# Hash-masked attention and a ReLU MLP on one core: value casts and sums leave GpSimd, row sums come out of the scaling, squares go to ScalarE

## The chip, the cores and the metric

The kernel runs on one core of a Trainium2 chip. Its engines are TensorE (PE in the profile; its weight loads are PEld), VectorE (DVE), ScalarE (ACT), GpSimd (POOL) and SyncE (SP), which only issues DMAs here. The metric is the device time of one execution in microseconds (us). The time before is 297.56 us, the median of three runs (296.8 to 298.05).

## The reference

The inputs are q, k and v of shape (4 batches, 8 heads, 768, 64), a projection to 6 hash bits, and the weights of an MLP (512 to 2048 to 512). A query sees a key only where all six hash bits agree.

```python
q_bits = (np.einsum('bhsd,dk->bhsk', q, proj) > 0)      # and k_bits likewise
mask = q_bucket[:, :, :, None] == k_bucket[:, :, None, :]
scores = np.where(mask, scale * np.matmul(q, k.transpose(0, 1, 3, 2)), -1e9)
attn = np.exp(scores - np.max(scores, axis=-1, keepdims=True))
attn = attn / (np.sum(attn, axis=-1, keepdims=True) + 1e-09)
attn_out = np.matmul(attn, v)
...
x = attn_out.transpose(0, 2, 1, 3).reshape(B, S, H * D)
xn = (x - mu) / np.sqrt(var + 1e-06) * g_ln             # mu, var over the 512 of a row
out = x + np.maximum(xn @ w_ch1, 0.0) @ w_ch2
```

## The kernel before

The work is cut into 12 units. Unit u is a third (256 rows) of the queries of batch u // 3, and has two groups g of four heads. All 768 keys are taken at once, in six blocks of 128. The code is a set of small functions, one for each step, and a long table ORDER of words such as `na.v.5.0`: step, engine (t TensorE, v VectorE, a ScalarE, p GpSimd, s SyncE), arguments (the unit, then the group or part). The program is the table read from left to right; each engine runs its own words in that order, one behind the other, and waits by semaphores for what it reads. A second table, SLOTS, gives each tile its buffer. So a word that waits holds everything behind it on its engine.

The steps, with their lines in the profile:

- Queries and keys of batches 1 to 3: `LX` loads them, `tu` turns them in 32x32 blocks (VectorE, L326), `CA` casts them to bf16 (L333 on ScalarE, L335 and L337 otherwise). `hm` projects them on TensorE (L547), `bt` makes bits of it (L329), and `mw` and `mr` send the bits through DRAM into tile G. Before, the keys' casts (`CA.p`, with 1 as the last argument) run on GpSimd.
- Values of a batch: `lv` loads them, `cv` casts them into vaug beside a column of ones (L495 or L497), `su` adds them over the key blocks in three passes (L502 to L504, GpSimd), `sp` sums that over the partitions with a matmul (L509), and `sc` copies the result into vsB (L522, L524).
- Attention: `S` multiplies the bits and then q and k (TensorE, L603), `E` takes the exponential (ScalarE, L620), `A` multiplies with the values (TensorE, L631). On VectorE, `na` adds a tiny multiple of the value sums (L643) and so frees the PSUM tile; `nb` takes the reciprocal of the row sum (L650) and scales (L652).
- Layer norm: `nc` takes the statistics (L656) and `ag` joins them (L659), both on VectorE; `rs` makes 1/sqrt of the variance on GpSimd, in two tiny instructions (L670, L671); `ce` subtracts and scales into xc (L665); `fl` is the transposing DMA into xnT (L674, SP's queue).
- First MLP product, in one of two ways. Plain (units 0 to 4 and 11): `F` on TensorE, eight parts of 8 matmuls that are 256 wide (L694), each evicted with the Relu by `R` (L702 on ScalarE, L704 on VectorE). By block products (units 5 to 10): `bs` adds input blocks (L736), `M` runs 14 parts of 8 matmuls that are 128 wide (L760), and `V` (L769, L771), `U` (L778), `Q` (L782, L784) and `ru` (L790, L792) combine the results on ScalarE and VectorE. These products need four sums of weight blocks, made once by `w1s` (L723).
- Second MLP product: `D` and `Z` in unit 0 (L797, L800), else by seven products `P` (L849) with input sums `ss` (L834) and additions `Y` to x (L854). `O` sends x out on SP's queue (L868; the last unit's at L866 also from ScalarE's).

PSUM has three two-bank tiles (tag pp) that S, A and unit 10's wide M share, and two one-bank tiles (tag f) for all else.

Of the kernel before, what the change touches and what calls it, by code (L numbers as in the profile page):

```python
# [38 lines left out]
tu.v.1.1.0.3 E.a.2.0.0.1 A.t.1.1.0.0 A.t.1.1.0.1 CA.p.1.0.1 na.v.1.1 nb.v.1.1 mr.s.1.0.2 mr.s.1.0.0  # L39
tu.v.1.1.0.1 tu.v.1.1.0.2 E.a.2.0.0.0 nc.v.1.0 F.t.0.2 R.a.0.2 S.t.2.0.2 S.t.2.0.3 E.a.2.0.1.1 su.p.1.0  # L40
# [17 lines left out]
tu.v.2.0.0.3 CA.a.2.0.0 Y.v.1.5 ss.v.1.3 S.t.4.0.2 ss.v.1.4 P.t.1.3 Y.v.1.6 Y.v.1.3 w1s.v.1.0 P.t.1.7 F.t.2.0
R.a.2.0 Y.v.1.7 nb.v.3.0 A.t.3.1.1.1 P.t.1.4 A.t.3.1.1.2 F.t.2.6 E.a.4.0.0.2 A.t.3.1.0.0 tu.v.2.0.1.1 Y.v.1.4
A.t.3.1.1.0 su.p.1.4 sp.t.1.4 E.a.4.0.0.0 A.t.3.1.0.2 A.t.3.1.0.1 nc.v.3.0 R.v.2.6 sc.a.1.4 na.v.3.1 nb.v.3.1  # L60
nc.v.3.1 ag.v.3.1 ag.v.3.0 F.t.2.2 R.v.2.2 S.t.4.0.3 N.a.4.0.1 S.t.4.0.4 E.a.4.0.1.1 S.t.4.0.5 O.s.0.3
E.a.4.0.1.2 hm.t.2.0 bt.v.2.0 E.a.4.0.1.0 O.s.1.0 CA.p.2.0.1 rs.p.3 ce.v.3.1 lv.s.2.0.0 O.s.0.1 lv.s.2.4.2
F.t.2.3 cv.a.2.0.0 ce.v.3.0 F.t.2.4 S.t.4.1.0 N.a.4.1.0 R.v.2.4 S.t.4.1.1 S.t.4.1.2 E.a.4.1.0.1 E.a.4.1.0.2
R.v.2.3 F.t.2.7 lv.s.2.4.0 O.s.1.1 R.a.2.7 F.t.2.5 fl.s.3.1 fl.s.3.0 O.s.1.3 A.t.4.0.0.1 A.t.4.0.1.0
E.a.4.1.0.0 LX.s.3.0.1 lv.s.2.4.1 lv.s.2.4.3 mw.s.2.0 O.s.1.2 tu.v.2.1.0.1 w1s.v.1.1 A.t.4.0.1.1 R.v.2.5
tu.v.2.1.0.0 ss.v.2.1 A.t.4.0.1.2 A.t.4.0.0.2 A.t.4.0.0.0 O.s.0.2 na.v.4.0 P.t.2.2 S.t.5.0.0 N.a.5.0.0
S.t.5.0.1 Y.v.2.2 S.t.5.0.2 E.a.5.0.0.1 E.a.5.0.0.2 E.a.5.0.0.0 P.t.2.1 ss.v.2.3 ss.v.2.2 F.t.3.6 Y.v.2.1
P.t.2.6 tu.v.2.1.1.0 ss.v.2.4 su.p.2.0 tu.v.2.1.1.3 R.v.3.6 S.t.4.1.3 N.a.4.1.1 S.t.4.1.4 E.a.4.1.1.1
S.t.4.1.5 tu.v.2.1.0.3 P.t.2.5 Y.v.2.6 P.t.2.7 Y.v.2.5 P.t.2.3 mr.s.2.0.1 Y.v.2.7 tu.v.2.1.1.2 E.a.4.1.1.0
# [119 lines left out]
def kernel(  # L189
# [16 lines left out]
    P = 128  # L206
# [706 lines left out]
```

## Time and profile before

| | |
|---|---|
| median of three runs | 297.56 us |
| the profiled execution, its own time | 299.32 us |
| its span on the core | 297.6 us |
| granted TensorE clock, mean | 0.999 |
| instructions in the profile, VectorE / ScalarE / GpSimd | 552 / 241 / 95 |
| chain that ended last: PE, DVE, issue, ACT, DMA | 74%, 17%, 3%, 3%, 1% |
| DMA traffic | 34.15 MB, mean 115 GB/s |

The busy line counts the time in which an engine runs something. Groups of instructions show line, engine, operation, out<-in, partitions x elements and type, their number, then the busy time in us and the mean of one in ns, and the idle time of the engine just ahead of them with what ended it. In the timeline each row is a run of equal instructions with start and length in us. TensorE's "idle" is time in which no matmul is under way.

### The profile page before, as it was taken

To read this page: it belongs to the slowest core of one execution; us is meant where nothing else is said; L and a number is where in the kernel's file an instruction comes from. 1 tells how busy PE (TensorE), PEld (TensorE's weight loads), DVE (VectorE), ACT (ScalarE), POOL (GpSimd) and SP (SyncE) were. 2 spreads that over 40 slices of the span, in tenths; PEclk is the share of its full clock that TensorE was granted. 3 is DMA by queue.
4 is the path that set the end of the run, shared out by engine and by line. 5 is a ranking of instruction groups with operands and counts; after the bars stand their busy time and mean duration, and the time that the engine had idled before them with its cause. 6 is when DMAs were issued, how large, how long until landed. Compare 5 with 4: busy or idle time off the path is not lost.

```text
span 297.6 us, 11168 instructions
## 1 busy us (share of the span) xinstructions
PE 282.2 (95%) x4879; PEld 227.9 (77%) x4879; DVE 247.8 (83%) x552; ACT 208.6 (70%) x241; POOL 64.8 (22%) x95
## 2 busy tenths in 40 slices
PE   8999999999999999999999999999899999977994
PEld 4777777558786885887887778788688879976883
DVE  4767899899988989999899898898698898986553
ACT  4789998987676755966766976887777985734140
POOL 4470415140511534202000235004101020010000
PEclk9999999999999999999999999999999999999999
DMA  6999896659905826417512022301200303012132
GB/s 198 367 288 269 190 276 115 135 176 175 326 16 144 240 63 220 103 29 195 150 32 68 12 70 65 73 3 37 55 20 20 71 22 56 4 35 63 24 111 72
DMA packets 31059, 34.15 MB, mean 115 GB/s; under 512 B 15521, under 2 KB 27809, under 8 KB 31010
## 3 DMA queue, kind: packets, MB, share of 16 engines
q1 hardware_dynamic: 25938, 28.72, 35.5%
q0 software_dynamic: 4224, 4.19, 8.6%
q8 instruction: 38, 0.62, 0.9%
q10 hardware_dynamic: 848, 0.53, 0.7%
q14 instruction: 11, 0.09, 0.1%
HBM read 27.86 MB, written 6.88 MB: 117 GB/s over the span
## 4 chain that ended last, share of the span: by engine, by line
PE 74%; DVE 17%; issue 3%; ACT 3%; DMA 1%; SPq 0%; POOL 0%; DVEq 0%; ACTq 0%
PE sc L603 14%; PE X L849 12%; PE f L694 11%; PE acc L631 10%; PE Yb L849 6%; PE Ma L760 6%; PE hf L415 3%; PE Me L760 3%; PE Ya L849 3%; ACT E L620 2%; PE hp L547 2%; PE Mae L760 2%; DVE xc L665 2%; DVE T L326 2%; DVE x L652 2%
## 5 line engine op out<-in xcount | busy, mean ns | idle before, releaser
L620 ACT ACTIVATE E<-sc,bias_sb 128x1024 bf16<-128x1024 f32 x144 | 152.4, 1115 | 39.6 <-PE sc L603 39.3
L603 PE MATMUL sc<-qb,kb 32*128 32x256 bf16 x1152 | 52.4, 267 | 0.0
L694 PE MATMUL f<-xnT,w_sb 128*128 128x256 bf16 x384 | 47.0, 273 | 1.2 <-DVE x L800 0.7
L603 PE MATMUL sc<-G 6*128 6x256 bf16 (+1 forms) x576 | 42.9, 272 | 2.6 <-ACT E L620 2.1
L694 PEld LDWEIGHTS <-w_sb 128*128 128x128 bf16 x384 | 36.0, 98 | 8.6 <-issue 4.8
L631 PE MATMUL acc<-vaug,E 128*128 128x65 bf16 x1152 | 42.3, 193 | 0.0
L631 PEld LDWEIGHTS <-E 128*128 128x128 bf16 x1152 | 40.2, 97 | 1.8 <-issue 0.4
L849 PEld LDWEIGHTS <-hb 128*128 128x128 bf16 x352 | 32.9, 98 | 8.3 <-issue 4.3
L603 PEld LDWEIGHTS <-kb 32*128 32x128 bf16 x1152 | 30.6, 93 | 1.3
L603 PEld LDWEIGHTS <-G 6*128 6x128 bf16 (+1 forms) x576 | 17.3, 91 | 16.9 <-issue 12.3
L849 PEld LDWEIGHTS <-S 128*128 128x128 bf16 x264 | 25.0, 98 | 5.3 <-issue 1.3
L702 ACT ACTIVATE hb<-f 128x512 bf16<-128x512 f32 x30 | 17.9, 601 | 15.6 <-PE f L694 14.2
L670 POOL TENSOR_SCALAR rs<-mv 128x2 f32<-128x2 f32 x12 | 3.0, 252 | 115.2 <-DVE mv L659 115.1
L326 DVE STREAM_TRANSPOSE T<-X 128x384 f32<-128x384 f32 (+2 forms) x52 | 26.4, 538 | 0.0
L643 DVE SCALAR_TENSOR_TENSOR y<-vsB,acc 128x520 f32<-128x520 f32 x24 | 16.6, 691 | 8.2 <-PE acc L631 7.4
L849 PE MATMUL Yb<-w_sb,S 128*128 128x256 bf16 x176 | 22.8, 273 | 0.5 <-DVE S L834 0.4
L854 DVE TENSOR_TENSOR x<-X,x 128x256 f32<-128x256 f32 x44 | 18.3, 419 | 5.1 <-PE X L849 4.5
L849 PE MATMUL X<-wt,hb 128*128 128x256 bf16 x168 | 21.8, 273 | 0.0
L652 DVE TENSOR_TENSOR x<-y,rc 128x512 f32<-128x512 f32 x24 | 20.1, 835 | 0.8
L760 PEld LDWEIGHTS <-Wx 128*128 128x128 bf16 x288 | 16.8, 98 | 4.0 <-issue 3.9
L760 PEld LDWEIGHTS <-w_sb 128*128 128x128 bf16 x288 | 16.9, 98 | 2.1 <-issue 2.0
L656 DVE BATCH_NORM_STATS2 st<-x 128x6 f32<-128x256 f32 x48 | 17.7, 412 | 0.2
(125 smaller groups left out, 433.9 us busy)
## 6 DMA issues: line engine op xcount, KB each, us to landing
out_dram<-x SPq DMA_DIRECT2D x45, 128.0 KB
X<-in_k_dram SPq DMA_DIRECT2D x7, 768.0 KB
vn<-in_v_dram SPq DMA_DIRECT2D x24, 192.0 KB
X<-in_q_dram SPq DMA_DIRECT2D x6, 768.0 KB
w_sb<-in_moe_w_ch_dram POOLq DMA_DIRECT2D x8, 512.0 KB, 11.0
vn<-in_v_dram SPq DMA_DIRECT2D x2, 768.0 KB
X<-in_q_dram SPq DMA_DIRECT2D x2, 512.0 KB
Bd<-B SPq DMA_DIRECT2D x6, 96.0 KB
```

The source lines that it names most:

```text
L326: nc.vector.transpose(d[:, j], s[:, j, kj0 : kj0 + n])
L603: m = nc.tensor.matmul(sc(u, g, a, p)[:, bank, 256 * half : 256 * half + 256], lh, rh, start=(rep == 0), stop=(rep == 2), skip_group_check ...
L620: nc.scalar.activation(Ep(u, g, a, p), sc(u, g, a, p), AF.Exp, scale=EXP_SCALE, bias=bias_sb)
L631: nc.tensor.matmul(acc[:, qt, (D + 1) * i : (D + 1) * (i + 1)], Ep(u, g, a, p)[:, bank, 256 * half + P * qt : 256 * half + P * qt + P], va ...
L643: nc.vector.scalar_tensor_tensor(yt(u, g), vs, EPS_ROW, made[f"acc{u}_{g}"][:, :, :A], op0=AOP.mult, op1=AOP.add,)
L652: nc.vector.tensor_tensor(xo, a[:, :, :, 0:D], rc.to_broadcast([P, 2, 4, D]), op=AOP.mult)
L656: nc.vector.bn_stats(stats(u)[:, qt, g], xt(u)[:, qt, 256 * g : 256 * g + 256])
L694: nc.tensor.matmul(f1[:, n].rearrange("p (t x) -> p t x", t=2), w1_sb[:, dt, P * nt : P * nt + P], xnT(u)[:, :, dt], start=(dt == 0), stop ...
L702: nc.scalar.activation(hb(u)[:, 2 * p : 2 * p + 2], f1, AF.Relu)
L760: nc.tensor.matmul(m[:, n], lh(kt)[:, P * nt : P * nt + P], rh[:, kt], start=(first and n == 0 and kt == 0), stop=(kt == 1), skip_group_ch ...
L849: nc.tensor.matmul(f2, lh[:, n], rh[:, n], start=(first and n == 0), stop=(n == 7), skip_group_check=True)
L854: nc.vector.tensor_tensor(x, made[f"{prod(u, k)}{u}"], x, op=AOP.add)
```

## The change

The kernel after does five things otherwise.

1. The key casts, value casts and value sums of batches 1 to 3 leave GpSimd. Of six key casts, three go to ScalarE and three to VectorE. Of the six value casts, the count on ScalarE rises from 4 to 10. All six value sums go to VectorE. GpSimd keeps batch 0's casts, the weight DMAs, the memsets of ones, and the tiny steps of the norm.
2. For units 3 to 11 the scaling `nb` becomes two scalar_tensor_tensor instructions that are 256 wide and also give each row's sum. `nc` and `ag` go for these units. A new step `mn` on GpSimd adds the two groups' sums and multiplies by -1/512, a new step `sv` on ScalarE squares x minus the mean and gives the sum of squares (what it writes into xc is overwritten by `ce`), and `rs` and `ce` read these.
3. Unit 4's first MLP product is made by block products: 40 parts F instead of 48, 98 parts M instead of 84.
4. Steps change engines: Relu evictions `R` go from 18 to 7 on VectorE and from 30 to 33 on ScalarE; `Q` from 1 to 7 on VectorE and 11 to 7 on ScalarE; `V` from 10 to 14 on VectorE and 26 to 28 on ScalarE; `U` on VectorE from 36 to 42.
5. ORDER and SLOTS are written anew from where unit 1's second half begins. The first 229 words are the same.

```diff
-tu.v.1.1.0.3 E.a.2.0.0.1 A.t.1.1.0.0 A.t.1.1.0.1 CA.p.1.0.1 na.v.1.1 nb.v.1.1 mr.s.1.0.2 mr.s.1.0.0
+tu.v.1.1.0.3 E.a.2.0.0.1 A.t.1.1.0.0 A.t.1.1.0.1 CA.a.1.0.1 na.v.1.1 nb.v.1.1 mr.s.1.0.2 mr.s.1.0.0
...
-WIDE = (10,)
+WIDE = {10}
+SUMS = 3
...
-        nc.vector.tensor_tensor(xo, a[:, :, :, 0:D], rc.to_broadcast([P, 2, 4, D]), op=AOP.mult)
+        if u < SUMS:
+            nc.vector.tensor_tensor(xo, a[:, :, :, 0:D], rc.to_broadcast([P, 2, 4, D]), op=AOP.mult)
+            return
+        for t in range(2):
+            nc.vector.scalar_tensor_tensor(
+                xo[:, t], a[:, t, :, 0:D], 1.0, rc[:, t].to_broadcast([P, 4, D]), op0=AOP.mult, op1=AOP.mult,
+                accum_out=rows(u)[:, g, t : t + 1],
+            )
+
+    def rows(u):
+        return sb(f"rw{u}", [P, 5, 2], F32, "rw", 3)
+
+    def mn(eng, u):
+        r = rows(u)
+        eng.tensor_tensor(r[:, 2], r[:, 0], r[:, 1], op=AOP.add)
+        eng.tensor_scalar(r[:, 3], r[:, 2], -1.0 / DM, None, op0=AOP.mult)
+
+    def sv(eng, u, t):
+        r = rows(u)
+        nc.scalar.activation(
+            xc(u)[:, t], xt(u)[:, t], AF.Square, bias=r[:, 3, t : t + 1], accum_out=r[:, 4, t : t + 1],
+        )
...
-        else:
+        elif u < SUMS:
...
+        else:
+            nc.vector.tensor_scalar(
+                xc(u)[:, t], xt(u)[:, t], rows(u)[:, 3, t : t + 1], rstd(u)[:, t : t + 1], op0=AOP.add, op1=AOP.mult,
+            )
...
-        nc.gpsimd.tensor_scalar(rstd(u), mv(u)[:, :, 1], 1e-6, None, op0=AOP.add)
+        if u < SUMS:
+            nc.gpsimd.tensor_scalar(rstd(u), mv(u)[:, :, 1], 1e-6, None, op0=AOP.add)
+        else:
+            nc.gpsimd.tensor_scalar(rstd(u), rows(u)[:, 4], 1.0 / DM, 1e-6, op0=AOP.mult, op1=AOP.add)
         nc.gpsimd.tensor_tensor(rstd(u), rstd(u), mhalf, op=AOP.pow)
```

In the rows below, a line number is that of the kernel the rows belong to (the one after is some 30 lines longer), and the number behind a name tells buffers of one name apart. First GpSimd's queue while batch 2 is made ready, before: key casts (kb), value sums (t, vsum) and value casts (vaug) of batch 2 stand between the norms (rs) of units 3 and 4.

```order
50 L337 CAST kb_2169<-T 128x1536
51 L670 TENSOR_SCALAR rs_2171<-mv_2097 128x2
52 L671 TENSOR_TENSOR rs_2171<-rs_2171,mhalf 128x2
53 L502 TENSOR_TENSOR t_2428<-vn_1820 128x512
54 L503 TENSOR_TENSOR t_2428<-t_2428,vn_1820 128x512
55 L504 TENSOR_TENSOR vsum_2431<-t_2428 128x256
56 L482 MEMSET vaug_2189 128x48
57 L483 MEMSET vsB_2639 128x8
58 L502 TENSOR_TENSOR t_2732<-vn_2178 128x512
```

The same queue after, from the norm of unit 3 on; rw is the new tile of row sums.

```order
40 L669 TENSOR_TENSOR rw_2039<-rw_2039 128x2
41 L670 TENSOR_SCALAR rw_2039<-rw_2039 128x2
42 L701 TENSOR_SCALAR rs_2190<-rw_2039 128x2
43 L702 TENSOR_TENSOR rs_2190<-rs_2190,mhalf 128x2
44 L485 MEMSET vaug_2193 128x48
45 L486 MEMSET vsB_2195 128x8
46 L669 TENSOR_TENSOR rw_2551<-rw_2551 128x2
47 L670 TENSOR_SCALAR rw_2551<-rw_2551 128x2
```

The wide passes are gone from it, and each norm has two more tiny ones ahead of the two that it had.

Second, ScalarE's queue while unit 6's scores come, before: E6 are unit 6's exponentials, hb4 the Relu evictions of unit 4's plain product, vsB2 a copy of value sums.

```order
114 L620 ACTIVATE E6_101_3189<-sc6_101_3153,bias_sb_66 128x1024
115 L702 ACTIVATE hb4_3167<-f1_44_3215 128x512
116 L702 ACTIVATE hb4_3167<-f1_45_3230 128x512
117 L702 ACTIVATE hb4_3167<-f1_47_3244 128x512
118 L702 ACTIVATE hb4_3167<-f1_46_3259 128x512
119 L702 ACTIVATE hb4_3167<-f1_40_3268 128x512
120 L620 ACTIVATE E6_102_3341<-sc6_102_3172,bias_sb_66 128x1024
121 L522 COPY vsB2_2639<-vp20_3304 128x4x64
122 L620 ACTIVATE E6_100_3368<-sc6_100_3150,bias_sb_66 128x1024
```

The same place after: kb30 is a key cast of batch 3, xc5 the squares of unit 5, and V4 are copies of unit 4's block products.

```order
126 L623 ACTIVATE E6_001_2997<-sc6_001_2945,bias_sb_66 128x1024
127 L336 ACTIVATE kb30_3021<-T_839 128x1536
128 L623 ACTIVATE E6_011_3128<-sc6_011_3103,bias_sb_66 128x1024
129 L623 ACTIVATE E6_012_3147<-sc6_012_3115,bias_sb_66 128x1024
130 L623 ACTIVATE E6_010_3177<-sc6_010_3100,bias_sb_66 128x1024
131 L674 ACTIVATE xc5_3218,rw5_3017<-x5_3016,rw5_3017 128x512
132 L800 COPY V460_3245<-Ma40_3166 128x512
133 L674 ACTIVATE xc5_3218,rw5_3017<-x5_3016,rw5_3017 128x512
134 L623 ACTIVATE E6_101_3265<-sc6_101_3195,bias_sb_66 128x1024
```

The evictions of unit 4 are gone from here, and the squares of unit 5 stand behind three exponentials and ahead of the next ones.

Third, VectorE's queue while batch 2's values are summed, after: t220 and vsum2 are the value sums, xc3 the normalised rows of unit 3, T the turned blocks of batch 2.

```order
143 L885 TENSOR_TENSOR x1_1008<-X1_1891,x1_1008 128x256
144 L329 STREAM_TRANSPOSE T_839<-X211_1750 128x384
145 L505 TENSOR_TENSOR t220_2165<-vn20_1657 128x512
146 L506 TENSOR_TENSOR t220_2165<-t220_2165,vn20_1657 128x512
147 L507 TENSOR_TENSOR vsum2_2168<-t220_2165 128x256
148 L754 TENSOR_TENSOR Wv1_2198<-w1_sb_75,Wx1_2015 128x1024
149 L693 TENSOR_SCALAR xc3_2142<-x3_2038,rw3_2039,rs3_2190 128x512 x2
150 L329 STREAM_TRANSPOSE T_839<-X210_2113 128x384 x2
```

The three passes of a value sum, before on GpSimd, now stand in VectorE's queue ahead of unit 3's normalised rows.

More of the change, by code (lines that the diff above doesn't have):

```diff
@@ new lines @@
+E.a.3.0.0.2 LX.s.2.0.1 mr.s.1.1.2 mr.s.1.1.0 nc.v.2.1 mr.s.1.1.3 D.t.0.0.2 D.t.0.1.1 D.t.0.1.2 D.t.0.1.3
+D.t.0.0.3 tu.v.2.0.0.0 mr.s.1.1.1 sw.v.3.0 ag.v.2.0 tu.v.2.0.0.2 ag.v.2.1 S.t.3.0.3 S.t.3.0.4 Z.v.0.0
+N.a.3.0.1 S.t.3.0.5 cv.a.1.0.0 lv.s.1.4.2 Z.v.0.1 E.a.3.0.1.1 F.t.1.1 R.a.1.1 wg.v.2 F.t.1.7 R.v.1.7
+E.a.3.0.1.0 F.t.1.0 E.a.3.0.1.2 rs.p.2 R.a.1.0 lv.s.1.4.1 F.t.1.6 lv.s.2.0.1 lv.s.1.4.0 tu.v.2.0.0.1 ce.v.2.1
+S.t.3.1.0 N.a.3.1.0 R.a.1.6 S.t.3.1.1 S.t.3.1.2 ce.v.2.0 w1s.v.1.1 tu.v.2.0.1.1 E.a.3.1.0.2 F.t.1.4
@@ new lines @@
+S.t.4.1.3 N.a.4.1.1 S.t.4.1.4 O.s.0.1 E.a.4.1.1.1 S.t.4.1.5 ss.v.2.4 tu.v.2.1.1.0 P.t.2.5 tu.v.2.1.0.1 Y.v.2.6
+ss.v.2.3 Y.v.2.5 P.t.2.7 su.v.2.4 mr.s.2.0.3 O.s.1.1 P.t.2.3 O.s.0.0 O.s.1.0 O.s.1.3 Y.v.2.3 E.a.4.1.1.0
+A.t.4.1.1.0 A.t.4.1.0.2 E.a.4.1.1.2 A.t.4.1.0.0 nb.v.4.0 A.t.4.1.1.1 A.t.4.1.1.2 A.t.4.1.0.1 na.v.4.1
+mr.s.2.0.2 Y.v.2.7 F.t.3.1 S.t.5.0.3 S.t.5.0.4 N.a.5.0.1 S.t.5.0.5 R.a.3.1 nb.v.4.1 w1s.v.3.1 mr.s.2.0.1
+E.a.5.0.1.2 P.t.2.4 Y.v.2.4 F.t.3.4 E.a.5.0.1.1 E.a.5.0.1.0 CA.v.2.1.1 hm.t.2.1 CA.v.2.1.0 cv.v.2.4.0
@@ new lines @@
+Y.v.6.6 cv.a.3.4.2 E.a.9.1.0.0 nb.v.8.1 P.t.6.3 P.t.6.7 A.t.9.0.0.1 A.t.9.0.1.2 A.t.9.0.1.0 Y.v.6.7 O.s.5.1
+bs.v.7.2 bs.v.7.4 Y.v.6.3 P.t.6.4 Y.v.6.4 bs.v.7.3 E.a.9.1.0.1 M.t.7.1.0 mn.p.8 sv.a.8.1 A.t.9.0.0.0
+A.t.9.0.0.2 A.t.9.0.1.1 V.a.7.1.0 na.v.9.0 M.t.7.2.0 U.v.7.1.0 M.t.7.6.0 S.t.9.1.4 S.t.9.1.3 sv.a.8.0
+V.a.7.6.0 nb.v.9.0 M.t.7.5.0 V.v.7.5.0 N.a.9.1.1 E.a.9.1.1.1 M.t.7.7.0 U.v.7.4.0 S.t.9.1.5 E.a.9.1.1.2
+M.t.7.3.0 U.v.7.2.0 E.a.9.1.1.0 M.t.7.4.0 S.t.10.0.0 N.a.10.0.0 Q.v.7.0 rs.p.8 ce.v.8.0 M.t.7.1.1 V.a.7.1.1
```

233 lines of the change are left out of this document (110 added, 123 removed).

## The prediction

> **What bounds the kernel now.** I read the page's busy line first, then the sums by stretch, then the timeline wherever TensorE stood still.
>
> ```profile
> PE 282.2 (95%) x4879; PEld 227.9 (77%) x4879; DVE 247.8 (83%) x552; ACT 208.6 (70%) x241; POOL 64.8 (22%) x95
> ...
> 40.00:260.00 220.00, 214.72 (x3924) 173.64 (x3917) 196.59 (x424) 165.18 (x188) 46.35 (x54) 1.00 0.40 97
> 88.00:153.00 65.00, 64.15 (x1085) 51.19 (x1084) 59.97 (x122) 44.76 (x52) 17.02 (x19) 1.00 0.49 135
> 260.00:276.00 16.00, 12.75 (x149) 11.22 (x147) 12.52 (x26) 6.11 (x10) 1.41 (x2) 1.00 0.23 50
> 276.00:293.30 17.30, 17.26 (x158) 15.18 (x156) 9.37 (x24) 4.79 (x8) 0.00 (x0) 1.00 0.21 56
> 293.30:297.60 4.30, 0.00 (x0) 0.00 (x0) 0.42 (x1) 0.00 (x0) 0.00 (x0) 0.96 0.44 119
> ```
>
> The columns behind each stretch are its length, then the busy time of TensorE's matmuls, of its weight loads, of VectorE, ScalarE and GpSimd, and the granted clock. TensorE is the bound: of the 220 us from 40 to 260 it is idle for 5.28, and from 276 until the last matmul for 0.04. VectorE is close behind, with 59.97 of 65 us busy from 88 to 153. ScalarE and GpSimd have room. So a gain has four possible sources: less TensorE work, the 5.28 us in the middle, the 3.25 us from 260 to 276, and the 4.30 us of output transfers at the end, which the change leaves alone. The first 40 us are the same in both kernels.
>
> **Who makes TensorE wait in the middle.** These are rows of the timeline: start, length, engine, line, operation; in brackets the idle time ahead of it and who ended that.
>
> ```profile
> 45.51 1.26 POOL L502 TENSOR_TENSOR t<-vn 128x512 f32<-128x512 f32 x1 [6.18 <-ACT E L620]
> 45.56 1.76 DVE L652 TENSOR_TENSOR x<-y,rc 128x512 f32<-128x512 f32 x1
> 52.57 1.50 PE L547 MATMUL hp<-T,p 128*32 128x384 f32 x16 [0.55 <-DVE T L326]
> 63.32 1.03 DVE L665 TENSOR_SCALAR xc<-x,mv,rs 128x512 bf16<-128x512 f32 x1
> 64.93 1.02 DVE L665 TENSOR_SCALAR xc<-x,mv,rs 128x512 bf16<-128x512 f32 x1
> 67.27 3.65 PE L694 MATMUL f<-xnT,w_sb 128*128 128x256 bf16 x32 [0.66 <-DVE x L800]
> 78.02 1.21 DVE L834 TENSOR_TENSOR S<-hb 128x1024 bf16<-128x1024 bf16 x1
> 79.89 0.38 PE L849 MATMUL X<-w_sb,hb 128*128 128x256 bf16 x2 [0.71 <-DVE hb L704]
> 110.31 1.54 DVE L652 TENSOR_TENSOR x<-y,rc 128x512 f32<-128x512 f32 x1
> 112.69 0.29 PE L603 MATMUL sc<-G 6*128 6x256 bf16 x4 [0.46 <-DVE y L643]
> 113.72 1.93 DVE L652 TENSOR_TENSOR x<-y,rc 128x512 f32<-128x512 f32 x1
> 116.17 1.03 PE L694 MATMUL f<-xnT,w_sb 128*128 128x256 bf16 x8 [0.23 <-DVE B L329]
> 176.06 1.75 DVE L834 TENSOR_TENSOR S<-hb,S 128x1024 bf16<-128x1024 bf16 x1
> 177.86 1.05 PE L849 MATMUL Yb<-w_sb,S 128*128 128x256 bf16 x8 [0.36 <-DVE S L834]
> L652 DVE TENSOR_TENSOR x<-y,rc x24: 691/692/1934, 24.4 to 256.6; 128x512 f32<-128x512 f32 x24
> L665 DVE TENSOR_SCALAR xc<-x,mv,rs x22: 501/541/1090, 59.7 to 266.3; 128x512 bf16<-128x512 f32 x22
> L834 DVE TENSOR_TENSOR S<-hb,S x12: 415/682/1748, 83.0 to 289.3; 128x1024 bf16<-128x1024 bf16 x10, 128x512 bf16<-128x512 bf16 x2
> ```
>
> The last three rows give minimum, median and maximum of one operation in ns. The same VectorE instruction takes 692 ns at the median and 1.54 to 1.93 us in these places, and in each of them a GpSimd sum or cast runs beside it (the first row is one). Each time a TensorE wait on VectorE follows: 0.55 + 0.66 + 0.71 + 0.46 + 0.23 + 0.36 = 2.97 us. The stretch ahead of each (1.07, 0.97, 0.53, 0.85, 1.24 and 1.07 us over the medians, 5.7 in all) is longer than the wait, but for the one at 78.02: of its 0.71 only 0.53 can be owed to the stretch.
>
> **The change part by part.** Prices of single instructions, by line and shape:
>
> ```profile
> L656 DVE BATCH_NORM_STATS2 st<-x 128x6 f32<-128x256 f32 x48 | 17.7, 412 | 0.2
> L659 DVE BATCH_NORM_AGGREGATE mv<-st 128x2 f32<-128x12 f32 x24 | 4.1, 192 | 0.2
> L704 DVE TENSOR_SCALAR hb<-f 128x512 bf16<-128x512 f32 x18 | 12.2, 681 | 1.7 <-PE f L694 1.5
> L778 DVE TENSOR_TENSOR hb<-Mb,V 128x512 bf16<-128x512 f32 x12 | 8.3, 688 | 4.2 <-PE Mb L760 3.0 <-ACT V L769 1.0
> L854 DVE TENSOR_TENSOR x<-X,x 128x256 f32<-128x256 f32 x44 | 18.3, 419 | 5.1 <-PE X L849 4.5
> L800 DVE SCALAR_TENSOR_TENSOR x<-f,rs,x 128x512 f32<-128x512 f32 x2 | 1.5, 740 | 0.0
> L335 DVE TENSOR_SCALAR qb<-T 128x1536 bf16<-128x1536 f32 x4 | 3.8, 938 | 0.0
> L620 ACT ACTIVATE E<-sc,bias_sb 128x1024 bf16<-128x1024 f32 x144 | 152.4, 1115 | 39.6 <-PE sc L603 39.3
> L702 ACT ACTIVATE hb<-f 128x512 bf16<-128x512 f32 x30 | 17.9, 601 | 15.6 <-PE f L694 14.2
> L333 ACT ACTIVATE qb<-T 128x1536 bf16<-128x1536 f32 x2 | 3.0, 1476 | 0.0
> L495 ACT CAST vaug<-vn 128x768 bf16<-128x768 f32 x4 | 3.4, 846 | 0.0
> ...
> 281.03 6.11 PE f L694 x56
> 255.77 2.27 PEld L760 LDWEIGHTS <-Wx 128*128 128x128 bf16 x40
> 259.78 0.27 DVE L659 BATCH_NORM_AGGREGATE mv<-st 128x2 f32<-128x12 f32 x2
> 260.14 0.28 POOL L670 TENSOR_SCALAR rs<-mv 128x2 f32<-128x2 f32 x1 [15.08 <-DVE mv L659]
> 266.84 1.19 SPq L674 DMA_TRANSPOSE xnT<-xc  x1
> 275.60 1.04 PE L694 MATMUL f<-xnT,w_sb 128*128 128x256 bf16 x8
> ```
>
> *Unit 4 on TensorE.* Eight groups of 8 matmuls go, at 6.11/56 = 0.109 us each: 64 x 0.109 = 6.98. Fourteen groups of 8 narrower ones come, at 2.27/40 = 0.057 each by their weight loads: 112 x 0.057 = 6.36; without the length of the last load in that row it is 6.24. TensorE saves 0.62 to 0.74; I take **-0.7 us**, and it counts in full where TensorE is the bound. The rest of unit 4 goes to engines beside it (below).
>
> *GpSimd's casts and sums.* The stretches vanish wherever a GpSimd pass did the stretching. I count the six waits above, **-2.8 us**, and nothing for the rest of the idle in the middle, since no stretch stands ahead of it in the rows shown. This assumes that the remade order has no more waits of its own than the old one. What hides the moved work is the slack of its new engine, so both loads have to be added up.
>
> *VectorE's load.* Gone: 36 statistics x 0.412 = 14.8, 18 aggregations x 0.192 = 3.5, 11 evictions x 0.681 = 7.5, and the stretches quoted, 5.7: together 31.5. New: 16 more evictions and additions of the block products x 0.688 = 11.0 (6 sums, 6 Relus, 4 copies); 3 key casts x 0.938 = 2.8; 6 value sums, each two 512-wide passes at 0.692 and one 256-wide at 0.419 = 10.8; 9 smaller passes of at most 0.42 (block inputs, Relu in place, value broadcast), 3.8: together 28.4. Then the row sums: 18 times a 512-wide product of 0.692 becomes two 256-wide ones that also sum. The trace has no summing instruction. Its nearest row is the 256-wide L854 at 0.419, which makes +0.15 each time and 2.6 in all; at L800's 0.740, a scalar_tensor_tensor of twice the width, it is 14.2. I take the former, since the width sets the time in the rows. VectorE ends 0.5 us lighter, or 11.1 heavier at the other end.
>
> *ScalarE's load.* Eighteen squares at L702's 0.601 for the same width = 10.8 (at the 1.115 of L620, twice as wide, 20.1); three key casts 4.4; six more value casts 5.1; evictions and copies shift by about nothing. That is +20 to +30 us over 208.6 of 297.6, and from 40 to 260 ScalarE is idle 54.8 of 220. Most of its idle is the 39.3 us that the exponentials wait for scores, so the cover is there; if it is gone, the scores' PSUM tiles are freed later and TensorE waits.
>
> *The new waits.* GpSimd now adds two row sums (L669, L670 of the new kernel), and a square on ScalarE waits for that; behind it in ScalarE's queue stand exponentials, on which the attention products wait. GpSimd's part is two instructions of about 0.28 with a hand-over ahead of each and behind. VectorE's aggregations ahead of 260.14 ended at 260.05, so a hand-over is 0.09: 0.8 us in all. Where an exponential of 1.1 us still stands ahead of the square, the wait costs nothing, and the rows of the order show one to three there in most units. The norm of a unit becomes longer by about this 0.8, plus two squares (1.2) less two statistics (0.8). In the last unit that has cover: its last transpose is issued at 266.84 and the first matmul that reads it ran at 275.60. The moved output and transpose DMAs on SP get no price: SP's queue waits for VectorE, not the other way round.
>
> *The tail.* I count nothing for it: its 3.25 us are waits between block products of unit 10 and their copies, by the timeline, and these stand in nearly the same order.
>
> Sum: -0.7 - 2.8 = -3.5 us. The profiled execution took 299.32 (span 297.6 and 1.72 around it), which would become 295.8. The median of the runs shown is 297.56, 1.76 below the profiled one, so I forecast 297.56 - 3.5 = **294.1 us**. A difference under 0.5%, 1.5 us, could not be told from no change.
>
> **The rivals.**
> *Slower: squares hold ScalarE's queue.* If GpSimd's two sums come so late that a square stands waiting, every exponential behind it is late. Price: the hand-over chain of 0.8 us in each of nine units, 7.2, where nothing of it is hidden, which is so only if TensorE's scores are already stopped for a free tile; less the 3.5 saved, +3.7: 301.3. With half of that hidden, it is 297.7. It decides when the sums land more than one exponential (1.1 us) after the last ScalarE instruction ahead of the square. For it: TensorE has 5.28 us of slack in 220, so lateness shows at once. Against it: 39.3 us of exponentials waiting for scores.
>
> *No change: the summing products are dear.* At 0.740 each VectorE gains 36 x 0.32 = 11.6 us; 12 of the 36 lie from 88 to 153, where VectorE has 5 us left and would spend 3.9 of them. TensorE's waits on VectorE stay, whoever stretches it: the 2.8 are not gained, and 0.7 is left: 296.9. Against it: the width governs every VectorE row above.
>
> [...]
>
> *More: the remade order takes out the other idle time too.* 5.28 + 3.25 + 0.7 = 9.2 us would give 288.3; half of what goes beyond my sum, 291.2. For it: no VectorE instruction is stretched any more. Against it: the tail's waits have no GpSimd in them (1.41 us busy there).
>
> *It doesn't do what it says:* TensorE stays packed, and another release is late next at each of the six places, such as ScalarE's with 20 us more; then -0.7: 296.9, with the no-change rival.
>
> **How the numbers follow.** The forecast (291.5 to 296) has 0.46; more, under 291.5, 0.10; the two no-change cases, 296.1 to 299, 0.24; slower, 0.20. Faster is 0.46 + 0.10 = 0.56. For 8 in 10 I leave out the larger part of "more" below 290.0 and the upper half of "slower" above 299.8. Those ends also take in the summing products at 0.740 and squares at 1.115.
>
> **What would show it.** Right: L652's, L665's and L834's counterparts have no instruction over 0.9 us past 50 us; TensorE idles some 2 to 3 us from 40 to 255; the 18 squares last near 0.6, with no exponential behind them held back. Wrong: summing products well over 0.42; ScalarE's idle time put down to GpSimd's row sums; TensorE idle with ScalarE's E as what ended the wait; a tail from the last score to the end that is longer than before.

## The result, and the profile after

The kernel after takes 294.35 us (median of 20 runs, 293.72 to 297.39), the one before 297.19 beside it (20 runs): ratio 0.9913, 95% interval 0.9894 to 0.9932. That is 2.8 us less; 294.1 was forecast. Its profiled execution took 293.72, with a span of 292.0. The profiled execution of before was 2.1 above its own median, so the two traces lie 5.6 us apart where the medians lie 2.8: totals below are medians, and the traces only say where. In four of the 20 runs the granted clock was 0.991 to 0.993 instead of 0.997 to 1.0, and these took 296.03 to 297.39 us; two experiments below (b7 and a4) have to be read with that.

The busy line of the page after, then the sums by stretch (length; busy time of TensorE's matmuls, of its weight loads, VectorE, ScalarE, GpSimd; granted clock).

```profile
PE 280.4 (96%) x4924; PEld 228.0 (78%) x4927; DVE 244.8 (84%) x587; ACT 228.9 (78%) x285; POOL 32.9 (11%) x83
...
40.00:260.00 220.00, 215.79 (x3973) 176.06 (x3965) 196.56 (x463) 186.68 (x235) 16.84 (x44) 1.00 0.38 96
88.00:153.00 65.00, 64.65 (x1128) 52.66 (x1121) 58.61 (x137) 52.60 (x68) 5.49 (x14) 1.00 0.48 128
260.00:276.00 16.00, 15.76 (x174) 14.13 (x173) 12.77 (x27) 4.46 (x7) 0.00 (x0) 1.00 0.18 34
276.00:287.40 11.40, 11.38 (x105) 9.95 (x102) 5.72 (x15) 4.18 (x7) 0.00 (x0) 1.00 0.32 83
```

The middle, 40 to 260, gave little: TensorE idles 4.21 us there instead of 5.28. By the timeline, its waits on VectorE fall from 3.7 us to 0.8, and those on ScalarE rise from 1.3 to 3.0. The tail, for which nothing had been counted, gave more: 0.24 us of idle instead of 3.25 in the 16 us from 260 on. GpSimd is busy for 32.9 us instead of 64.8, and ScalarE for 20.3 us more.

Groups of instructions after, by line (busy us, mean ns, idle before):

```profile
L659 DVE SCALAR_TENSOR_TENSOR x<-y,rc 128x256 f32<-128x256 f32 x36 | 13.9, 422 | 0.6
L659 DVE DVE_READ_ACCUMULATOR x<-y,rc 128x1 f32 x36 | 2.9, 81 | 0.0
L693 DVE TENSOR_SCALAR xc<-x,rw,rs 128x512 bf16<-128x512 f32 x18 | 9.4, 533 | 0.4 <-POOL rs L702 0.4
L674 ACT ACTIVATE xc<-x,rw 128x512 bf16<-128x512 f32 x18 | 12.9, 718 | 0.8 <-DVE vsum L507 0.5 <-PE sc L606 0.3
L674 ACT ACTIVATION_READ_ACCUMULATOR xc<-x,rw 128x1 f32 x18 | 3.5, 192 | 0.0
```

The summing product takes 422 ns, where the plain sum of two tensors of its width took 419 before (L854), with a second instruction of 81 behind it; a square takes 0.72 + 0.19 us. None of the squares' idle time is put down to GpSimd's row sums.

TensorE's three longest waits past 40 us after, in the timeline, and ScalarE just before the second of them:

```profile
52.21 1.50 PE L550 MATMUL hp<-T,p 128*32 128x384 f32 x16 [0.60 <-DVE T L329]
152.39 0.37 ACT L525 COPY vsB<-vp 128x256 f32<-128x256 f32 x1 [2.21 <-PE vp L512]
154.01 0.59 ACT L800 COPY V<-Ma 128x512 f32<-128x512 f32 x1 [1.24 <-DVE x L885]
157.97 0.29 PE L606 MATMUL sc<-G 6*128 6x256 bf16 x4 [1.27 <-ACT E L623]
187.43 0.29 PE L606 MATMUL sc<-G 6*128 6x256 bf16 x4 [1.09 <-ACT E L623]
```

In the last two, 1.27 and 1.09 us, the scores wait for an exponential to free a tile. Ahead of the one at 157.97 ScalarE had itself stood 2.21 and 1.24 us. The kernel before has one wait of this kind in the middle, elsewhere in its order:

```profile
210.38 0.29 PE L603 MATMUL sc<-G 6*128 6x256 bf16 x4 [1.30 <-ACT E L620]
```

And the three waits of before's tail (its timeline), which have no counterpart over 0.25 us after:

```profile
263.81 0.61 PE L760 MATMUL Mae<-bs,Wx 128*128 128x128 bf16 x8 [1.16 <-ACT V L769]
268.34 0.61 PE L760 MATMUL Mae<-xnT,Wv 128*128 128x128 bf16 x8 [0.85 <-DVE hb L778]
273.71 1.03 PE L849 MATMUL Ya<-w_sb,hb 128*128 128x256 bf16 x8 [1.23 <-DVE hb L778]
```

### The profile page after: what moved, and what is told of

Same layout as the page of the kernel before. It is cut to its first block, busy times and chain, and to the rows that moved or that the text cites. A ratio compares the mean times of both kernels' runs of the same rounds, so it can differ in the third digit from the quotient of the medians.

```text
span 292.0 us, 11314 instructions
## 1 busy us (share of the span) xinstructions
PE 280.4 (96%) x4924; PEld 228.0 (78%) x4927; DVE 244.8 (84%) x587; ACT 228.9 (78%) x285; POOL 32.9 (11%) x83
## 4 chain that ended last, share of the span: by engine, by line
PE 84%; DVE 7%; ACT 6%; issue 1%; DVEq 0%; ACTq 0%
PE sc L606 17%; PE X L880 12%; PE acc L634 11%; PE f L725 10%; PE Ma L791 7%; PE Yb L880 6%; ACT E L623 4%; PE Ya L880 3%; PE Me L791 3%; PE hp L550 3%; PE hf L418 3%; PE f L828 2%; PE Mb L791 2%; PE warm L388 1%; DVE T L329 1%
## 5 line engine op out<-in xcount | busy, mean ns | idle before, releaser
L634 PE MATMUL acc<-vaug,E 128*128 128x65 bf16 x1152 | 43.1, 193 | 0.4 <-ACT E L623 0.4
L725 PE MATMUL f<-xnT,w_sb 128*128 128x256 bf16 x320 | 38.8, 273 | 0.4 <-ACT hb L733 0.2
L725 PEld LDWEIGHTS <-w_sb 128*128 128x128 bf16 x320 | 30.2, 98 | 5.4 <-issue 2.1
L733 ACT ACTIVATE hb<-f 128x512 bf16<-128x512 f32 x33 | 19.6, 599 | 13.5 <-PE f L725 10.5
L791 PEld LDWEIGHTS <-w_sb 128*128 128x128 bf16 x336 | 20.2, 97 | 3.0 <-issue 2.8
L791 PEld LDWEIGHTS <-Wx 128*128 128x128 bf16 x336 | 19.6, 98 | 2.3 <-issue 2.1
L669 POOL TENSOR_TENSOR rw<-rw 128x2 f32<-128x2 f32 x9 | 2.1, 237 | 139.1 <-DVE x L659 139.1
L791 PE MATMUL Ma<-bs,Wx 128*128 128x128 bf16 x192 | 14.7, 219 | 0.0
L659 DVE SCALAR_TENSOR_TENSOR x<-y,rc 128x256 f32<-128x256 f32 x36 | 13.9, 422 | 0.6
```

What stands on the lines that cost most here:

```text
L634: nc.tensor.matmul(acc[:, qt, (D + 1) * i : (D + 1) * (i + 1)], Ep(u, g, a, p)[:, bank, 256 * half + P * qt : 256 * half + P * qt + P], va ...
L659: nc.vector.scalar_tensor_tensor(xo[:, t], a[:, t, :, 0:D], 1.0, rc[:, t].to_broadcast([P, 4, D]), op0=AOP.mult, op1=AOP.mult, accum_out=r ...
L725: nc.tensor.matmul(f1[:, n].rearrange("p (t x) -> p t x", t=2), w1_sb[:, dt, P * nt : P * nt + P], xnT(u)[:, :, dt], start=(dt == 0), stop ...
L733: nc.scalar.activation(hb(u)[:, 2 * p : 2 * p + 2], f1, AF.Relu)
L791: nc.tensor.matmul(m[:, n], lh(kt)[:, P * nt : P * nt + P], rh[:, kt], start=(first and n == 0 and kt == 0), stop=(kt == 1), skip_group_ch ...
```

## The experiments

Theory A is the prediction's: GpSimd's passes stretch VectorE's instructions, and TensorE waits for those. Theory B: the remade order is the gain. Theory C: VectorE's load as such. The b runs start from the kernel before and add a part; the a runs start from the kernel after and take one away. Where an edit makes a tile's turn come otherwise, its letter in SLOTS follows; that is not shown. Ratios are to the kernel before, timed beside each run on the same chip (medians 297.27 to 297.48).

### Parts alone, in the old order

**b1**, only the casts and sums moved:

```diff
-CA.p.1.0.1 ... su.p.1.0 ... CA.p.1.1.1 ... su.p.2.4 ... cv.p.2.4.0 ... cv.p.2.4.2
+CA.a.1.0.1 ... su.v.1.0 ... CA.v.1.1.1 ... su.v.2.4 ... cv.v.2.4.0 ... cv.a.2.4.2
```

> The kernel before, with the key casts, value casts and value sums of batches 1 to 3 on the engines of the kernel after, in the old order; norm, unit 4 and tail as before. Theory A (the prediction: the six TensorE waits in the middle follow VectorE instructions stretched by GpSimd, and go with its passes): 294.4 to 296, no VectorE instruction of lines 652, 665 or 834 over 0.9 us past 50 us, TensorE idle under 4 us of the 220 from 40 to 260, the tail's three waits still there. Theory B (the gain comes from the remade order, the engine alone decides nothing): 296.7 to 298.5, since VectorE (60 of 65 us busy from 88 to 153 before) takes the sums at their old places and TensorE waits for it there as much as before.

Measured: 311.91 us, ratio 1.0483 (1.0458 to 1.0507). It lies 13 us above the slower of the two forecasts. In its trace TensorE's waits from 40 to 260 come to 14.1 us instead of 5.0; the rest of the 14.6 was not traced (the granted clock was 0.987 to 0.989). VectorE and then TensorE in its timeline:

```profile
120.53 0.64 DVE L500 TENSOR_TENSOR t<-vn 128x512 f32<-128x512 f32 x1
121.20 0.69 DVE L501 TENSOR_TENSOR t<-t,vn 128x512 f32<-128x512 f32 x1
121.93 0.43 DVE L502 TENSOR_TENSOR vsum<-t 128x256 bf16<-128x256 f32 x1
122.27 0.95 DVE L335 CAST kb<-T 128x1536 bf16<-128x1536 f32 x1
126.98 0.29 PE L601 MATMUL sc<-G 6*128 6x256 bf16 x4 [2.50 <-DVE y L641]
142.85 1.03 PE L692 MATMUL f<-xnT,w_sb 128*128 128x256 bf16 x8 [3.30 <-DMA xnT<-xc]
```

On GpSimd these passes could stand together, as little was behind them. On VectorE they stand ahead of a unit's norm and of the step that frees a scores tile (y), and TensorE waits 2.50 us. The 3.30 us come another way. A value cast of batch 2, first on GpSimd in the kernel before and then on ScalarE in b1:

```profile
120.28 0.84 POOL L497 CAST vaug<-vn 128x768 bf16<-128x768 f32 x1
136.07 0.84 ACT L493 CAST vaug<-vn 128x768 bf16<-128x768 f32 x1
SPq L487 <- ACT vaug L493: 13.2, 1, 13.2
```

At its old place in the table it now stands behind exponentials and runs some 16 us later. SyncE's queue waits 13.2 us for it (the last row, from the view of waits) with a load of values, and the transposes that TensorE needs stand behind that load.

**b2**, only the norm by row sums:

```diff
-nc.v.4.1 ... nc.v.4.0 ag.v.4.1 ag.v.4.0 S.t.5.1.2 E.a.5.1.0.2
+mn.p.4 S.t.5.1.2 E.a.5.1.0.2 sv.a.4.1 sv.a.4.0
```

> The kernel before, with only the norm of units 3 to 11 by row sums and squares; GpSimd keeps its casts and sums, old order. VectorE gets lighter by some 12 us (36 statistics x 0.41 and 18 aggregations x 0.19 less 36 x 0.5 for what was 18 x 0.69). Theory A: within 0.7 us of before (296.5 to 298), as TensorE's waits stem from the stretched instructions. Theory C (VectorE's load as such made the waits): 294.5 to 296. Rival (squares behind GpSimd's wide passes hold ScalarE's queue): 298 to 300, with ScalarE idle ahead of squares.

Measured: 312.3 us, 1.0497 (1.0459 to 1.0535). GpSimd, VectorE and TensorE in its timeline:

```profile
117.65 1.46 POOL L336 CAST kb<-T 128x1536 bf16<-128x1536 f32 x1
119.06 0.83 POOL L496 CAST vaug<-vn 128x768 bf16<-128x768 f32 x1
119.98 0.19 POOL L697 TENSOR_SCALAR rs<-rw 128x2 f32<-128x2 f32 x1
121.00 1.02 DVE L689 TENSOR_SCALAR xc<-x,rw,rs 128x512 bf16<-128x512 f32 x1 [3.89 <-POOL rs L698]
123.60 0.29 PE L602 MATMUL sc<-G 6*128 6x256 bf16 x4 [2.02 <-DVE y L642]
```

It is a cousin of the prediction's slower rival. One square waits for GpSimd, for 1.6 us, but VectorE waits 7.0 us in four places: here the norm's second half lies in GpSimd's queue behind casts, VectorE stands 3.89 us, and what frees the scores' tile stands behind it. The row sums put twice as many steps on GpSimd, four a norm, and here they stand behind its casts.

**b3**, both of these edits:

```diff
-su.p.2.4 ... nc.v.5.1 ... ag.v.5.1 ... ag.v.5.0
+su.v.2.4 ... mn.p.5 ... sv.a.5.1 ... sv.a.5.0
```

> The kernel before with both: casts and sums off GpSimd, and the norm by row sums; old order, unit 4 plain, old tail. Theory A: 294 to 295.5 (the middle's -1.4 to -2.8). Theory B: 296.5 or more. If b1 is slower for VectorE's load and this is faster, the row sums are what makes room for the moved casts.

Measured: 315.84 us, 1.0642 (1.0602 to 1.0682), worse than either. All of the change, in its own order, takes 294.35; two of its parts in the old order cost 18.6 us. So b1 to b3 do not price the parts, but they show that words of this table that change their engine need new places.

### GpSimd alone

**b5** empties GpSimd without loading anyone. DMAs on SyncE's queue, of other data of the same shape, stand for its casts and sums of batches 1 to 3, which this kernel leaves out.

```diff
+        if eng is nc.sync:
+            eng.dma_start(out=qk(t, b, g), in_=qk(0, b, g))
+            return
...
-CA.p.1.1.1 ... su.p.2.4 ... CA.p.2.1.1 cv.p.2.4.0
+CA.s.1.1.1 ... su.s.2.4 ... CA.s.2.1.1 cv.s.2.4.0
```

> The kernel before with nothing moved but GpSimd's wide passes of batches 1 to 3 gone: DMAs on SP's queue, of other data of the same shape, stand in for the key casts, value casts and value sums that GpSimd did (the values are then wrong, the work of all other engines is the same). It measures what GpSimd's passes cost where they stood, without new load on VectorE or ScalarE. Theory A (stretched VectorE instructions make TensorE's waits in the middle): 294.2 to 296, no instruction of lines 652, 665 or 834 over 0.9 us past 50 us, TensorE idle 2.5 to 4 us from 40 to 260 where before had 5.28. Theory B (order): 296.8 to 297.6. A later arrival by DMA than by GpSimd would show as TensorE waiting for vaug, vsum or kb.

Measured: 298.92 us, 1.0051 (1.0033 to 1.0069): not faster, but by waits of the stand-in, 3.35 us for transposes that its DMAs held up in SyncE's queue and 0.95 for kb. So **b7** puts five of these DMAs elsewhere:

```diff
-su.s.2.4 ... CA.s.2.1.1 cv.s.2.4.0 ... mw.s.2.1 ... cv.s.2.4.2 ... fl.s.4.1 fl.s.4.0
+mw.s.2.1 su.s.2.4 CA.s.2.1.1 ... fl.s.4.1 fl.s.4.0 cv.s.2.4.0 cv.s.2.4.2
...
-CA.a.1.1.0 ... CA.s.1.1.1
+CA.a.1.1.0 CA.s.1.1.1
```

> As b5 (before, with DMAs of other data in place of GpSimd's passes), with five of those DMAs put at other places in SP's queue: the key cast of batch 1 earlier, four of batch 2 behind the transposes or bits they held up. In b5 (298.92) TensorE stood 3.35 us for the transposes of unit 4 and 0.95 us for kb, both waits of the stand-in; its other idle from 40 to 260 was 2.24 against 5.28. Theory A: without those two waits it takes 294 to 295.3. Theory B: 296.7 to 297.6, and TensorE's idle turns up elsewhere.

Measured: 296.38 us, 0.9967 (0.9943 to 0.999). Its 12 runs are split by the granted clock: five at 1.0 took 294.8 to 295.12 (median 294.95), seven at 0.994 took 296.31 to 297.75. Of the 23 runs of before beside it, 22 were at 0.997 or more, median 297.42. At like clocks it is 2.5 us faster, within what theory A expected, with a wait of the stand-in's own (the first row) and the old tail still in its timeline:

```profile
65.98 4.60 PE L700 MATMUL f<-xnT,w_sb 128*128 128x256 bf16 x40 [2.03 <-DMA xnT<-xc]
...
260.05 0.61 PE L766 MATMUL Mae<-bs,Wx 128*128 128x128 bf16 x8 [1.16 <-ACT V L775]
```

No VectorE instruction past 40 us is over its usual time by 0.2 us or more (VectorE is busy for 191.00 us from 40 to 260 where before had 196.59), and TensorE's waits on VectorE from 40 to 260 are 0.6 us instead of 3.7; the tail's waits are as they were. The other way round, **a1**: the kernel after with idle passes on GpSimd where its work had left it.

```diff
+    def ju(eng, kind, b, x):
+        thin = made["scrB"]
+        wide = lambda n: made["scrF"][:, :].unsqueeze(1).to_broadcast([P, n // 16, 16])
...
-su.v.3.0
+su.v.3.0 ju.p.2.3.0
```

> The kernel after with idle work on GpSimd: at each of the 18 places where a cast or sum left GpSimd it now makes passes of about the same length on a small tile of its own that nobody reads. Everything else is the kernel after. Theory A: VectorE instructions beside them are stretched to 1.0 to 1.9 us again, and it takes 295.5 to 297.2 (+1.2 to +2.8). Theory B: 294 to 294.9.

Measured: 297.72 us, 1.0011 (0.9993 to 1.0029); 3.4 over the kernel after, more than its whole gain of 2.8 (GpSimd is busy for 75.3 us here, for 64.8 in the kernel before). VectorE, GpSimd and TensorE at one such place:

```profile
178.42 1.09 DVE L507 TENSOR_TENSOR t<-vn 128x512 f32<-128x512 f32 x1
179.55 1.20 DVE L508 TENSOR_TENSOR t<-t,vn 128x512 f32<-128x512 f32 x1
178.14 3.08 POOL L557 TENSOR_TENSOR scrB<-scrF 128x384 bf16<-128x384 f32 x3
181.88 0.27 PE L514 MATMUL vp<-vsum,ones 128*128 128x256 bf16 x1 [0.99 <-DVE x L898]
```

Nobody reads what GpSimd makes here; the sums on VectorE, 0.68 and 0.69 us each in the kernel after, take 1.09 and 1.20, and TensorE waits 0.99. The passes do not act by holding up GpSimd's own steps of the norm: VectorE waits 0.4 us for those, as in the kernel after, and no square waits for them; in the view of TensorE's waits none is put down to GpSimd. Theory A's mechanism is shown in both kernels: the stretches go with the passes in b7, and come back with idle ones here. By what they stretch them is not shown.

### The norm and unit 4, taken back

**a2**, statistics in place of the row sums in the kernel after:

```diff
-nb.v.9.0 ... nb.v.9.1 ... mn.p.9 sv.a.9.1 ... sv.a.9.0 rs.p.9
+nb.v.9.0 nc.v.9.0 ... nb.v.9.1 ... nc.v.9.1 ag.v.9.1 ag.v.9.0 ... rs.p.9
```

> The kernel after with the norm of units 3 to 11 by statistics as before, each statistics instruction right behind the scaling that it reads and no squares on ScalarE; order else unchanged. VectorE gets some 12 us more, ScalarE 16 less. By the prediction's sum the row sums were worth nothing by themselves: 293.8 to 295. Theory C (the room on VectorE is what the gain rests on): 297 or more, with TensorE waiting for VectorE's copies and sums.

Measured: 302.02 us, 1.0157 (1.0136 to 1.0178), 7.7 over the kernel after, as theory C has it. The order was not remade for the statistics, so this holds for this order alone. TensorE's waits in a2 (total us, times, longest):

```profile
PE Ma L789 <- DVE hb L807: 1.3, 4, 0.6
PE Yb L878 <- DVE x L883: 1.1, 2, 0.8
PE vp L510 <- DVE B L330: 0.8, 1, 0.8
PE sc L604 <- DVE y L644: 0.7, 2, 0.4
```

Many small waits on VectorE, all over the program.

**a4**, unit 4's first product plain in the kernel after:

```diff
-M.t.4.1.0 V.v.4.1.0 ... M.t.4.6.0 ... M.t.4.7.0 U.v.4.4.0
+F.t.4.1 R.v.4.1 ... F.t.4.0 R.a.4.0 ... F.t.4.3 R.a.4.3
```

> The kernel after with unit 4's first MLP product plain: 8 F parts and 8 Relu evictions (2 on VectorE, 6 on ScalarE) at the places of the 14 M parts and their copies and sums. TensorE gets 0.7 us more, VectorE some 10 us less, ScalarE 2 us more. By the prediction's term: 294.8 to 295.4 (+0.7). If VectorE's room is worth more there than TensorE's 0.7: 293 to 294.3.

Measured: 297.04 us, 0.9992 (0.9974 to 1.0011), 2.7 over the kernel after, though VectorE has less to do. Eight of its 12 runs were at a clock of 0.994 to 0.996; the four at 0.997 or more have a median of 296.3, 2.3 over that of the kernel after's 16 (294.05). Two waits are new in TensorE's timeline:

```profile
140.46 0.42 PE L630 MATMUL acc<-vaug,E 128*128 128x65 bf16 x8 [0.97 <-POOL rs L698]
147.86 1.03 PE L876 MATMUL X<-w_sb,hb 128*128 128x256 bf16 x8 [0.78 <-DVE hb L731]
```

They are 1.75 us; that they come from the places where the Relus were put was not tested. What is left, about 0.5 at like clocks, is near the 0.7 for TensorE but does not settle it.

### The tail

**b4**, the kernel before up to 245 us, then after's order and engines (seven copies and Relus differ in theirs), the norm by statistics:

```diff
-P.t.9.5 P.t.9.6 P.t.9.3 M.t.10.7.0 M.t.10.3.0 M.t.10.2.0 P.t.9.7
+P.t.9.5 M.t.10.6.1 P.t.9.6 M.t.10.7.1 M.t.10.7.0 P.t.9.3 M.t.10.4.1 M.t.10.3.0 M.t.10.2.0 P.t.9.7
```

(TensorE's words alone.) Where the old order has three output products of unit 9 in a row and then block products of unit 10 that each wait for a copy, the new one lays the former between the latter.

> The kernel before up to the last scores of unit 11 (245 us), and from there the order and engines of the kernel after, with the old norm by statistics. By the prediction the tail's order is worth nothing: 297 to 297.6. By the two traces (TensorE's 3.25 us of idle from 260 to 276 before, 0.29 after): 293.8 to 294.8, with no wait over 0.4 us between block products of units 9 and 10.

Measured: 298.56 us, 1.0041 (1.0023 to 1.0059). The three waits are gone, but six others came, 3.94 us from 242 on, five of them on VectorE. **b6** adds the row sums of units 10 and 11 to it:

```diff
-nc.v.10.0 ... nc.v.10.1 ag.v.10.1 ag.v.10.0 ... nc.v.11.1 ag.v.11.1 ag.v.11.0
+mn.p.10 ... sv.a.10.0 ... sv.a.10.1 ... mn.p.11 ... sv.a.11.0 ... sv.a.11.1
```

> As b4 (the kernel before, and from 245 us the order of the kernel after), but with the norm of units 10 and 11 by row sums as in the kernel after. If the tail's gain of 3.2 needs VectorE freed of statistics: 293.8 to 295, with no wait of TensorE on VectorE over 0.5 us past 240. If the tail's order needs the whole state that the kernel after enters it with: 297 or more, as b4 (298.56).

Measured: 295.91 us, 0.9952 (0.9934 to 0.9969): 1.4 less than before, from the tail alone; unlike the kernel after it still waits 0.5 and 0.7 us ahead of unit 11's first product. **a5** is the opposite, the kernel after with the old order and engines from unit 11's last scores on, row sums kept:

```diff
-P.t.9.5 M.t.10.6.1 P.t.9.6 M.t.10.7.1 M.t.10.7.0 P.t.9.3 M.t.10.4.1 M.t.10.3.0 M.t.10.2.0 P.t.9.7
+P.t.9.5 P.t.9.6 P.t.9.3 M.t.10.7.0 M.t.10.3.0 M.t.10.2.0 P.t.9.7
```

> The kernel after up to the last scores of unit 11 (240 us), and from there the order and engines of the kernel before, the norm still by row sums. The prediction counted the tail's order as nothing: 294 to 294.8, with before's three waits gone because VectorE is lighter. If the order itself holds the three waits (3.24 us between the block products of units 9 and 10 in before): 296.5 to 298, with those waits back at the same instructions.

Measured: 301.18 us, 1.014 (1.0116 to 1.0165). In its timeline:

```profile
242.85 1.13 PE L632 MATMUL acc<-vaug,E 128*128 128x65 bf16 x32 [1.28 <-ACT E L621]
263.22 0.61 PE L789 MATMUL Mae<-bs,Wx 128*128 128x128 bf16 x8 [1.22 <-ACT V L798]
267.74 0.61 PE L789 MATMUL Mae<-xnT,Wv 128*128 128x128 bf16 x8 [0.85 <-DVE hb L807]
273.11 1.03 PE L878 MATMUL Ya<-w_sb,hb 128*128 128x256 bf16 x8 [1.23 <-DVE hb L807]
```

The old tail brings its three waits back at the same instructions with a lighter VectorE: 1.22 + 0.85 + 1.23 = 3.30 us. The order, with its engines, holds them. The rest of the 6.8 us over the kernel after are other waits of this graft, as the 1.28 at 242.85.

### The waits that are left

**a3** attacks TensorE's waits at 157.97, 187.43 and 52.21 in the kernel after:

```diff
-P.t.4.3 ... P.t.4.7 A.t.6.1.1.0 A.t.6.1.1.2 sp.t.2.4 A.t.6.1.1.1 sc.a.2.4 ... P.t.4.4 M.t.5.1.0 ... na.v.6.1 ... S.t.7.0.3
+A.t.6.1.1.0 A.t.6.1.1.2 A.t.6.1.1.1 ... na.v.6.1 ... P.t.4.3 ... S.t.7.0.3 ... P.t.4.7 ... P.t.4.4 M.t.5.1.0
...
-sp.t.2.0 sc.v.2.0
+sp.t.2.0 sp.t.2.4 sc.v.2.0
...
-E.a.8.1.1.2 S.t.9.0.0 N.a.9.0.0 Q.a.6.0 M.t.6.1.1 CA.v.3.1.1
+E.a.8.1.1.2 Q.v.6.0 M.t.6.1.1 CA.v.3.1.1 S.t.9.0.0 N.a.9.0.0
...
-hm.t.1.1 S.t.2.1.4 S.t.2.1.5 D.t.0.0.0
+D.t.0.0.0 hm.t.1.1 S.t.2.1.4 S.t.2.1.5
```

> The kernel after with its two longest TensorE waits attacked (1.27 us at 157.97 and 1.09 at 187.43, both for an exponential that frees a scores tile) and a third of 0.60 at 52.21. Unit 6's attention products go ahead of unit 4's second product, so that unit 7's scores start some 2 us earlier and ScalarE has work; batch 2's two value sums share one tile and one copy; a Relu of unit 6 goes to VectorE and TensorE's next block product ahead of unit 9's scores; unit 0's first output product goes ahead of the hash product of batch 1. If the waits are what they look like: 291.6 to 292.8. If the idle time moves to the next release: 293.8 to 294.8. If VectorE, at 84%, becomes late: over 295.

Measured: 293.99 us, 0.9885 (0.9865 to 0.9904), beside 0.9913 (0.9894 to 0.9932) for the kernel after: the fastest here, but not to be told from it. TensorE in its timeline:

```profile
65.33 0.29 PE L603 MATMUL sc<-G 6*128 6x256 bf16 x4 [0.30 <-ACT E L620]
157.81 0.29 PE L603 MATMUL sc<-G 6*128 6x256 bf16 x4 [0.41 <-ACT E L620]
161.09 0.61 PE L788 MATMUL Ma<-bs,w_sb 128*128 128x128 bf16 x8 [0.44 <-DVE hb L806]
188.21 0.29 PE L603 MATMUL sc<-G 6*128 6x256 bf16 x4 [0.36 <-ACT E L620]
```

The long waits are cut to a third, and shorter ones stand beside them. TensorE's idle time from 40 to 260 is 3.09 us instead of 4.21 in the trace, but the medians are only 0.36 apart: part of the idle time went to the next release, and what became of the rest is not shown.

## Why the prediction was right in its total, and where its steps failed

- **GpSimd's passes, -2.8 us: right.** b7 found 2.5 us for them in the old kernel at like clocks, a1 3.4 in the new one. TensorE's waits on VectorE fall by 2.9 us in the traces; of the six that were counted five are gone, and the one for T is still there (0.60 at 52.21). But the size rests on one execution, 2.1 us above its kernel's median: in the traces of b4 and b6, whose code is before's up to 245 us, the same six waits come to 2.0 and 2.4. After, no instruction of lines 656, 659, 693 or 865 is stretched past 50 us.
- **"This assumes that the remade order has no more waits of its own than the old one": wrong.** Two waits on exponentials, 1.27 and 1.09 us, stand against one of 1.30 in the kernel before, and TensorE's waits on ScalarE grow by 1.7 in all. So the 220 us of the middle idle 1.07 us less, not 2.8, and 4.2 remain where 2 to 3 were forecast. It is what the rival "it doesn't do what it says" named, another release that is late next. Whether ScalarE's 20 us more load makes these waits stays open: ahead of the one at 157.97 ScalarE itself stood, and a3 shows only that cutting them pays next to nothing.
- **"I count nothing for it", the tail: the step that failed most.** Its waits may "stand in nearly the same order", but the words that differ are the ones that hold them. The trace has 3.0 us less idle there, so the rival "more" was right on this point. a5 shows that the order holds the three waits, b4 and b6 that it pays only with VectorE relieved by the row sums: +1.3 without, -1.4 with them.
- **The row sums, nothing by themselves: wrong as a way of counting.** Their prices were put too low, above all because both have a second instruction: a summing product with its accumulator read takes 0.50 us (422 + 81 ns) for 0.419 forecast, a square 0.91 (0.72 + 0.19) for 0.601. The loads came out near all the same: ScalarE rose by 20.3 us of +20 to +30, and VectorE fell by 3.0 instead of 0.5. But a2 puts the loss without them at 7.7 us in this order, and in the tail they are worth 2.7 (b4 to b6): a load spread over a nearly full engine is not judged by a few named waits.
- **The no-change rival by dear summing products fell.** They take 422 ns for 256 elements, not L800's 740; the plain sum of two tensors of that width (L854) takes 419. The width alone did not set every row of the kernel before, though: L834's 1024 elements of bf16 took 682 ns at the median, L704's 512 out of f32 681.
- **The slower rival** did not come true after, but b2 shows its kind at 15 us where GpSimd keeps its casts.
- **Unit 4, -0.7:** the price of the parts holds. In TensorE's timeline after, block products that wait for nothing start 0.45 us apart, 14 of them 6.2 us, where 8 plain parts were put at 7.0:

```profile
252.97 0.61 PE L791 MATMUL Ma<-bs,Wx 128*128 128x128 bf16 x8
253.42 0.61 PE L791 MATMUL Me<-bs,Wx 128*128 128x128 bf16 x8
253.86 0.61 PE L791 MATMUL Mae<-bs,Wx 128*128 128x128 bf16 x8
```

  As time of the whole, a4 neither confirms nor refutes it.

So that the forecast lies 0.25 us off the median is luck: a tail of some -3 that was left out stands for a middle that gave less. Of the traces' 5.6 us, about 1.0 is the start alone, the same code in both (the first exponential begins at 9.35 us before and 8.39 after).

## What to carry to other kernels

In a table of fixed queues an instruction's price is also what stands behind it: moving GpSimd's work to ScalarE and VectorE cost 15 us (b1) where its words kept their places. Test such a part from both sides, by adding idle work to the fast kernel and by taking work out of the slow one, rather than by moving it alone. And read a tail that is said to stay "in nearly the same order" instruction by instruction: in a5 the old one brought waits of 1.22, 0.85 and 1.23 us back.

## What was not expected of the hardware

In the trace of the kernel after, an accumulated output comes as an instruction of its own: 81 ns on VectorE (L659), 192 on ScalarE (L674). In a1, passes of GpSimd that read 16 elements over and over stood beside a sum on VectorE that took 1.20 us instead of 0.69; beside wide casts and sums in the kernel before, L652 took 1.54 to 1.93 us instead of 0.692.
